# An mLSTM with an MLP behind it: Softplus and Erf on ScalarE, gate exponents read back from DRAM, a 512-token up projection, and a list schedule

## The chip, the cores and the metric

The kernel runs on one core of a Trainium2 chip. The metric is the device time of one execution in microseconds (us), less being better. The kernel before was run three times: 509.87, 509.98 and 510.92 us, median 509.98.

## What is computed

An mLSTM layer (batch 4, 8 heads, 768 tokens, head size 40) is followed by a two-layer MLP on all 3072 tokens. In short form (all data are float32; the weights reach the chip as float64 words):

```python
def _attn_ref(q, k, v, i_gate, f_gate, o_gate):
    ...
    for t in range(S):
        m_new = np.maximum(f_gate[:, :, t] + m, i_gate[:, :, t])
        f_stab = np.exp(f_gate[:, :, t] + m - m_new)
        i_stab = np.exp(i_gate[:, :, t] - m_new)
        C = f_stab[..] * C + i_stab[..] * np.einsum('bhd,bhe->bhde', vt, kt)
        n = f_stab[..] * n + i_stab[..] * kt
        denom = np.maximum(np.abs(nq), 1.0)          # nq = n . q
        o = 1.0 / (1.0 + np.exp(-o_gate[:, :, t]))
        y[:, :, t] = o * (C q) / denom

def _moe_ref(x, w_in, w_out):                        # x 3072 x 320
    h = x @ w_in                                     # 320 x 2048
    sp = np.maximum(h, 0.0) + np.log1p(np.exp(-np.abs(h)))   # softplus
    return (h * erf(sp)) @ w_out                     # 2048 x 320
```

## The kernel before

**Attention.** The 768 tokens are worked off in 6 chunks of `L` = 128. A step `s` is one chunk `c` of one batch `b`, so there are 24 steps. For a chunk, `gate_chunk` runs the scans of the gates on VectorE and leaves rows `x0`: a decayed input exponent, a decay exponent, and its exponential. To spread these rows over 128 partitions, each row is split into three bf16 parts and multiplied by rows of ones: L503 (and L505 in chunk 0) adds the two exponents in PSUM with 512 columns for half of the heads, ScalarE takes `Exp` into `dm` (L510), and GpSimd masks it. L548 does the same for the factor on `q` and on the state. The scores are L536 (32 small matmuls), the product with the mask is L526, the output `ph` is L564 and L568, and the state's increment `pk` is L579 from `vg`. `den` is the denominator, `y` is the gated output in `kvo`, written by L608 and L615. Three transposes (L624) turn `y` into columns; ScalarE copies the rounded part `xh` (L633), VectorE subtracts the remainder `xl` (L637). A pair of batches fills 256 tokens.

**MLP.** A group `g` is 1024 elements a partition: 4 column blocks `j` of `w_in` by 256 tokens; 48 groups do all. An operand is held as a rounded float32 part and a remainder, so an up block is eight matmuls of 256 columns for each `j` (L769). ScalarE copies `h` out of PSUM to `hb` (L779) and evaluates erf(softplus(h)) by an approximation of four `Tanh` passes and a `Square` (L785, L789, L793, L798, L810) with two passes on VectorE between them (L802, L806). VectorE multiplies by `h` (L814), rounds to `gh` (L819) and subtracts to `gl` (L824). The down block is three matmuls of 320 columns for each `j` and batch (L838, L839, L841) into the banks `po0` and `po1`; after the fourth group ScalarE scales them out (L847).

**Weights.** Each weight tile comes as pairs of 32-bit words; ScalarE and VectorE make float32 of them (L654, L659, L660, L662), ScalarE rounds (L667), and the remainder is taken by VectorE (L680) or, for `w_out`, by two matmuls with the identity (L674, L675) and a copy (L682). Raw words lie in MLP tiles that are not yet in use (`raw_tile`) or in tiles named `raw`.

**Order.** Every piece of work is put into a list with a time from tables of numbers (`ATT`, `MLP`, `LOAD`, `DECODE`, `GROUP_AT` and others), the list is sorted by that time, and this is the order of each engine's instructions. Each engine takes its instructions in this order and waits for what each one needs. SyncE (SP) issues all DMAs. PSUM has four banks for attention (`pa`), two for `h`, and one each for `po0` and `po1`.

```python
        def put(fn):
            plan.append((start + parts[part], len(plan), fn))
...
    with tc.manual_schedule():
        for _, _, fn in sorted(plan, key=lambda x: x[:2]):
            fn()
```

## Time and profile before

| what | value |
|---|---|
| time, median of 3 runs | 509.98 us (509.87 to 510.92) |
| span of the profiled execution | 508.03 us, 15222 instructions |
| that execution's own time | not listed apart from the three runs |
| ScalarE table loads | 1 |
| DMA | 39.48 MB, mean 78 GB/s |

The span is what the hardware profiler saw from the first to the last instruction; the time of a run is a little longer. PE is TensorE's matmuls and PEld its weight loads, DVE is VectorE, ACT is ScalarE, POOL is GpSimd. A page of the profile divides the span into 40 slices and gives each engine's busy share there; views of the trace give windows, groups of like instructions, and single rows. A row of the timeline is the start in us, the duration, the engine, the line, the operation with its output and inputs, and shapes. A group has the count behind an x, then its busy sum, the mean of one in ns, and the idle time before it.

### The profile page before, as it was taken

Reading aid. Unit: us, or ns where it says so; the run is one execution under the profiler, and the core shown is the slowest. Engines: PE = TensorE matmul, PEld = TensorE weight load, DVE = VectorE, ACT = ScalarE, POOL = GpSimd, SP = SyncE. Lnnn points to the kernel's source line nnn. Section 1 sums busy time; section 2 is a strip of 40 time slices with the busy share of each in tenths; the row PEclk is TensorE's granted clock in tenths of the full one; section 3 lists DMA queues with packets and bytes.
Section 4 is the critical chain, followed back from the end, with each engine's and each line's share of the span. In section 5 each row is a group of like instructions: output and inputs, shape, how many; then the busy total and the mean of one; then the engine's idle time right before and its main releaser. Section 6 shows DMA issues by size and latency. Waiting matters only on the chain.

```text
span 508.0 us, 15222 instructions
## 1 busy us (share of the span) xinstructions
PE 471.2 (93%) x6552; PEld 440.5 (87%) x6552; DVE 444.7 (88%) x695; ACT 382.5 (75%) x616; POOL 88.6 (17%) x112
## 2 busy tenths in 40 slices
PE   3647889998999999999999999999999999999996
PEld 2435689897998999999999999999999999999995
DVE  5879999999997989988989989989989878787873
ACT  6556889877778868868768878768769679678980
POOL 3212002113222113113013113013113013010000
PEclk9865899999999999999999999999999999999999
DMA  7949713303205012212113114104015004000000
GB/s 249 259 166 229 230 56 111 89 3 108 78 5 160 15 46 72 69 38 96 46 46 93 47 39 126 49 3 131 10 39 158 16 3 139 1 15 15 0 28 26
DMA packets 16811, 39.48 MB, mean 78 GB/s; under 512 B 2728, under 2 KB 7336, under 8 KB 16744
## 3 DMA queue, kind: packets, MB, share of 16 engines
q1 hardware_dynamic: 16744, 38.51, 26.2%
q8 instruction: 51, 0.84, 0.7%
q14 instruction: 16, 0.13, 0.1%
HBM read 33.40 MB, written 3.93 MB: 73 GB/s over the span
## 4 chain that ended last, share of the span: by engine, by line
PE 55%; DVE 23%; ACT 8%; DMA 7%; issue 4%; SPq 2%; DVEq 0%; ACTq 0%
PE h L769 22%; PE po L838 8%; PE po L841 7%; PE po L839 7%; PE pa L536 4%; DVE gl L824 3%; DVE n L802 3%; DVE hb L814 3%; DVE n L806 3%; DMA qk<-in_qk_dram 3%; PE pa L564 2%; PE pa L568 2%; DMA hb<-in_w_in_dram 2%; DVE gh L819 2%; ACT n L810 2%
## 5 line engine op out<-in xcount | busy, mean ns | idle before, releaser
L769 PE MATMUL h<-xh,wh 128*128 128x256 f32 x576 | 161.7, 286 | 1.2 <-ACT n L785 1.2
L769 PE MATMUL h<-xl,wh 128*128 128x256 f32 x576 | 160.2, 283 | 1.7 <-DVE xl L637 1.7
L838 PE MATMUL po<-woh,gh 128*128 128x320 f32 x384 | 123.5, 331 | 2.7 <-DVE gh L819 1.5
L839 PE MATMUL po<-wol,gh 128*128 128x320 f32 x384 | 114.6, 308 | 0.0
L769 PEld LDWEIGHTS h<-xh,wh 128*128 128x128 f32 x576 | 109.9, 191 | 2.3 <-ACT n L785 1.4
L769 PEld LDWEIGHTS h<-xl,wh 128*128 128x128 f32 x576 | 109.8, 191 | 2.3 <-DVE xl L637 2.2
L769 PE MATMUL h<-xh,wl 128*128 128x256 f32 x384 | 108.5, 283 | 0.0
L841 PE MATMUL po<-woh,gl 128*128 128x320 f32 x384 | 82.4, 315 | 0.8 <-DVE gl L824 0.8
L838 PEld LDWEIGHTS po<-woh,gh 128*128 128x128 f32 x384 | 72.4, 189 | 6.1 <-DVE gh L819 2.1
L839 PEld LDWEIGHTS po<-wol,gh 128*128 128x128 f32 x384 | 72.3, 188 | 1.2 <-issue 0.6
L769 PEld LDWEIGHTS h<-xh,wl 128*128 128x128 f32 x384 | 73.3, 191 | 0.0
L785 ACT ACTIVATE n<-h 128x512 f32<-128x512 f32 x96 | 57.8, 606 | 19.5 <-PE h L769 17.8
L618 POOL COPY kvo<-kvo 128x64 f32<-128x64 f32 x24 | 22.8, 950 | 258.5 <-DVE kvo L615 101.5
L814 DVE SCALAR_TENSOR_TENSOR hb<-n,hb 128x1024 f32<-128x1024 f32 x48 | 59.5, 1239 | 7.2 <-ACT n L810 6.9
L824 DVE TENSOR_TENSOR gl<-hb,gh 128x1024 fp32r<-128x1024 f32 x48 | 60.7, 1265 | 4.5 <-DVE gh L819 0.5
L841 PEld LDWEIGHTS po<-woh,gl 128*128 128x128 f32 x384 | 59.6, 188 | 1.6 <-DVE gl L824 1.2
L806 DVE SCALAR_TENSOR_TENSOR n<-n,n 128x1024 f32<-128x1024 f32 x48 | 58.9, 1228 | 2.3
L802 DVE SCALAR_TENSOR_TENSOR n<-n,hb 128x1024 f32<-128x1024 f32 x48 | 58.4, 1217 | 2.9 <-ACT n L793 2.9
L779 ACT ACTIVATE hb<-h 128x512 f32<-128x512 f32 x96 | 53.0, 604 | 10.1 <-DVE gl L824 10.1
L810 ACT ACTIVATE n<-n 128x1024 f32<-128x1024 f32 x48 | 50.8, 1058 | 10.5 <-DVE n L806 10.2
L514 POOL TENSOR_SCALAR_AFFINE_SELECT dm<-dm 128x512 f32<-128x512 f32 x48 | 44.9, 944 | 54.2 <-ACT dm L510 54.2
L793 ACT ACTIVATE n<-n 128x1024 f32<-128x1024 f32 x48 | 50.9, 1061 | 1.3
(92 smaller groups left out, 730.8 us busy)
## 6 DMA issues: line engine op xcount, KB each, us to landing
kvo<-in_kvo_dram SPq DMA_DIRECT2D x24, 484.0 KB
...
```

What stands on the lines that cost most here:

```text
L769: nc.tensor.matmul(v.h[n // 2][:, n % 2 * T:(n % 2 + 1) * T], w, m, start=(q == 0), stop=(q == len(ops) - 1))
L779: nc.scalar.activation(v.hb[:, hs], v.h[i], AF.Copy)
L785: nc.scalar.activation(v.a[:, hs], v.h[i], AF.Tanh, scale=PARAMS[0], bias=PARAMS[1])
L793: nc.scalar.activation(v.a, v.a, AF.Square, scale=PARAMS[6], bias=PARAMS[7])
L802: nc.vector.scalar_tensor_tensor(out=v.a, in0=v.a, scalar=PARAMS[8], in1=v.hb, op0=ALU.add, op1=ALU.mult)
L806: nc.vector.scalar_tensor_tensor(out=v.a, in0=v.a, scalar=PARAMS[9], in1=v.b, op0=ALU.mult, op1=ALU.add)
L810: nc.scalar.activation(v.a, v.a, AF.Tanh, scale=PARAMS[10], bias=PARAMS[11])
L814: nc.vector.scalar_tensor_tensor(out=v.hb, in0=v.a, scalar=1.0, in1=v.hb, op0=ALU.add, op1=ALU.mult)
L824: nc.vector.tensor_tensor(v.gl, v.hb, v.gh.bitcast(F32), op=ALU.subtract)
L838: nc.tensor.matmul(po[k, b], v.gh[:, ts], woh[:, w], start=(j == 0), stop=False)
L839: nc.tensor.matmul(po[k, b], v.gh[:, ts], wol[:, w], start=False, stop=False)
L841: nc.tensor.matmul(po[k, b], v.gl[:, ts], woh[:, w], start=False, stop=(j == NFF - 1))
```

## The change

Four parts are exchanged. The line numbers in this section are those of the changed kernel, where the piece is new.

**Gate exponents.** No bf16 split and no replication matmul is left. In a step of chunk 0 the rows are spread by 16 float32 matmuls with a column of the identity broadcast (L403, L404). From chunk 1 on, GpSimd and TensorE have no part in it: the decay rows and their exponentials are written to DRAM (`gd`) and read back replicated over the partitions, as `dm` and `eT`; the input exponent comes from one transpose of the rows (L354, `aT`) and is added by VectorE (L427) ahead of `Exp` (L431). VectorE multiplies `q` (L469) and the state (L503) by `eT`.

**Steps.** The denominator is four short VectorE passes; `y` is turned by two transposes and, for the last 64 columns, two float32 matmuls on halves of the array (L542, L544).

**MLP.** In chunk 0 a group is as before, 4 `j` by 256 tokens. From chunk 1 on it is 2 `j` by 512 tokens, all four batches at once (L691), with a PSUM bank `po` for each batch. ScalarE evaluates `Softplus` (L703) and `Erf` (L708); VectorE multiplies (L713), rounds (L717), subtracts (L721). `Exp`, `Softplus` and `Erf` lie in three table sets of ScalarE (X, S, G), and each change of the set is an instruction of its own, `ACT_TABLE_LOAD`, on ScalarE (L769): 59 in the program. Groups go in pairs: two groups' `Softplus`, a change of the set, their two `Erf`.

**Weights and order.** Raw words have three tiles of their own (`raw`) and are decoded in place; `w_in` and `w_out` come by quarters of the 2048 columns, and every second `w_out` block leaves its remainder to TensorE and ScalarE, the other to VectorE. The tables are gone: `Plan` gives each piece an engine, an estimated cost, and due times that follow backwards from a nominal time of each group, and simulates the engines to choose, at each moment, the piece with the earliest due time whose inputs and tiles are there.

```diff
-GROUP_EVERY = 14.1101
...
+class Plan:
...
+    LAT = {'PE': 0.15, 'ACT': 0.2, 'DVE': 0.15, 'POOL': 0.2, 'SP': 0.0}
+    SWITCH = 1.5
+    RATE = 240e3
...
+    def dues(self):
...
+        for _ in range(3):
+            for o in reversed(self.ops):
+                for s in o.succ:
...
+                    if phase < len(todo) and loaded != phase:
+                        k = self.kinds[phase]
+                        if loaded is None or self.kinds[loaded] != k:
+                            order.append((now, lambda k=k: switch(k)))
+                            free[e] = now + self.SWITCH
...
+                    if o.phase is not None and o.phase != phase or o.sets and self.kinds[loaded] not in o.sets:
+                        continue
...
+                    due = o.due - (1.0 if e == 'PE' and o.kind == mode else 0.0)
+                    if best is None or due < best[0]:
+                        best = (due, o)
...
+KIND = {'X': 'exp_and_others', 'S': 'softplus', 'G': 'sigmoid_and_others'}
+BATCHES = [[2, 2, 2, 2]] * 6
+SLOTS = dict(gt=1, m=2, x=2, aT=2, qk=2, kvo=2, dm=2, eT=1, vg=1, den=2, xh=2, xl=2, o=2,
+             raw=3, hb=4, n0=4, gh=2, gl=2, pa=2, h=2, gd=2, **{f'po{b}': 1 for b in range(B)})
+START = 30.0
...
+SLOW = 9.0
...
+def nominal(g):
+    return START + (SLOW * g if g < 8 else SLOW * 8 + EVERY * (g - 8))
+EVERY = 8.6
...
+    for c in range(NC):
+        g = 8 * c
+        for i, n in enumerate(BATCHES[c]):
+            if c + 1 < NC and i in XAT[c > 0]:
+                exps[c + 1][XAT[c > 0].index(i)] = plan.phase('X')
+            s = plan.phase('S')
+            e = plan.phase('G')
+            for j in range(n):
+                soft[g + j], erfs[g + j] = s, e
...
+            nc.tensor.transpose(p[:, 0:128], t['x', c][:, 0], ident)
...
+        @op('ACT', 0.22, r=[(('x', c), 0)], w=[(('x', c), 2)], phase=exps[c - 1][1])
+        def _():
+            nc.scalar.activation(t['x', c][:, 2], t['x', c][:, 1], AF.Exp)
...
+                    t['gd', c] = tc.dram_tile([2, B, H, L], F32, name=f"gd{c}")
+                nc.sync.dma_start(t['gd', c][:, b].rearrange("i h t -> h i t"), t['x', c][32 * b:32 * b + H, 1:3])
...
+                        k = 32 * b + 4 * i + h
+                        one = ident[:, k:k + 1].to_broadcast([128, 128])
+                        nc.tensor.matmul(p[:, h], one, t['x', c][:, 1], start=True, stop=False)
+                        nc.tensor.matmul(p[:, h], t['x', c][:, 0], one, start=False, stop=True)
...
+                    nc.scalar.activation(A('dm')[:, 4 * i:4 * i + 4], A(f'pb{i}').rearrange("p (h t) -> p h t", t=L), AF.Exp)
...
+            @dma(512, r=[(('gd', c), b)], w=[K('dm', 'e0'), K('dm', 'e1')], tile_=('dm', ('dm', s)))
+            def _():
+                nc.sync.dma_start(new('dm', [128, H, L], ('dm', s)).rearrange("p h t -> p (h t)"),
+                                  t['gd', c][0, b].rearrange("h t -> (h t)").partition_broadcast(128))
...
+                nc.sync.dma_start(e[0:64], src[0].partition_broadcast(64))
+                nc.sync.dma_start(e[64:QR], src[1].partition_broadcast(D))
...
+            @op('DVE', 1.18, r=[(('aT', c), 0)], w=[K('dm', 'e0'), K('dm', 'e1')])
+            def _():
+                nc.vector.tensor_tensor(A('dm'), A('dm'), bias().to_broadcast([128, H, L]), op=ALU.add)
...
+            @op('ACT', 0.95, w=[K('dm', 'e0'), K('dm', 'e1'), K('dm', 0), K('dm', 1)], phase=ph)
+            def _():
+                nc.scalar.activation(A('dm'), A('dm'), AF.Exp)
...
-                for p in range(NPR):
-                    nc.tensor.matmul(pq[:, p], selP[:, 2 * p:2 * p + 2].rearrange("p a b -> p (a b)"),
-                                     splB[b][:, 1, :], start=True, stop=True)
...
+            @op('DVE', 0.6, r=[K('eT')], w=[K('qk', 'q')])
+            def _():
+                q = A('qk')[0:QR, 0]
+                nc.vector.tensor_tensor(q, q, A('eT')[0:QR], op=ALU.mult)
...
+            nc.vector.tensor_copy(den, pv()[:, :, D])
+            nc.vector.scalar_tensor_tensor(out=den, in0=den, scalar=-1.0, in1=den, op0=ALU.mult, op1=ALU.max)
+            nc.vector.tensor_scalar(out=den, in0=den, scalar1=1.0, scalar2=2.0, op0=ALU.max, op1=ALU.mult)
+            nc.vector.reciprocal(den, den)
...
+            for i in range(2):
+                nc.tensor.transpose(p[:, i * L:(i + 1) * L], y[:, i * 128:(i + 1) * 128], ident)
+            for i in range(2):
+                nc.tensor.matmul(p[64 * i:64 * i + 64, 2 * L:3 * L], y[:, 256:320], ident, start=True, stop=True)
...
+        @op('DVE', n / 960 + 0.1, r=r, w=[(R, 1)])
+        def _():
+            nc.vector.tensor_scalar(out=raw()[:, :, 0], in0=raw()[:, :, 0], scalar1=29, scalar2=None,
+                                    op0=ALU.logical_shift_right)
...
+            lo_, hi_ = raw()[:, :, 0], raw()[:, :, 1]
+            nc.vector.scalar_tensor_tensor(out=lo_, in0=hi_, scalar=3, in1=lo_,
...
+            nc.vector.scalar_tensor_tensor(out=lo_, in0=hi_, scalar=-0x80000000, in1=lo_,
                                            op0=ALU.bitwise_and, op1=ALU.bitwise_or)
...
+        if by_dve:
+            @op('DVE', n / 960 + 0.1, r=[(R, 1), whi], w=[wlo])
...
+                nc.vector.tensor_tensor(lo(), word(0), hi().bitcast(F32), op=ALU.subtract)
+        else:
...
+            @op('PE', 0.85 * n / 320, r=[(R, 1), whi, ('ident', 0), ('nident', 0)], w=[(z, 0)], tile_=('pa', z), kind='a')
...
+            @op('ACT', n / 1200 + 0.06, r=[(z, 0)], w=[wlo])
...
+            raw_of[R] = raw(R, 2 * DM)
+            nc.sync.dma_start(raw_of[R], w_out.bitcast(I32)[j * 128:(j + 1) * 128])
...
+               ('woh', j), ('wol', j), j % 2 == 0)
...
+        js, bs = (range(4 * (q // 2), 4 * (q // 2) + 4), range(2 * (q % 2), 2 * (q % 2) + 2)) if c == 0 else \
+            (range(2 * q, 2 * q + 2), range(B))
...
+        per = 512 // N
...
+                    for k, (w, m) in enumerate(ops):
+                        nc.tensor.matmul(h[:, n * N:(n + 1) * N], w, m, start=(k == 0), stop=(k == len(ops) - 1))
...
+        @op('ACT', 0.95, r=[(('hb', g), 0), (('hb', g), 1)], w=[(('n0', g), 0)], tile_=('n0', ('n0', g)), phase=soft[g])
+        def _():
+            nc.scalar.activation(new('n0', [128, 1024], ('n0', g)), G('hb'), AF.Softplus)
...
+        @op('ACT', 0.95, w=[(('n0', g), 0)], phase=erfs[g])
...
+            nc.scalar.activation(n0, n0, AF.Erf)
...
+            nc.vector.tensor_tensor(n0, n0, G('hb'), op=ALU.mult)
...
+        for b in bs:
...
+                        if lo:
+                            nc.tensor.matmul(po, a[:, ts], woh[:, j], start=False, stop=(j == NFF - 1))
+                        else:
+                            nc.tensor.matmul(po, a[:, ts], woh[:, j], start=(j == 0), stop=False)
+                            nc.tensor.matmul(po, a[:, ts], wol[:, j], start=False, stop=False)
...
+    order = plan.run(nc.scalar.preload_act_table_set and (lambda k: nc.scalar.preload_act_table_set(KIND[k])))
...
     with tc.manual_schedule():
-        for _, _, fn in sorted(plan, key=lambda x: x[:2]):
+        for fn in order:
             fn()
```

On TensorE, late in the program, before: the last `L548` matmuls of a step, down blocks of two groups, and the next step's replication (`selP` and `splB` hold the selecting rows and the split exponents).

```order
L548 LDWEIGHTS selP
L548 MATMUL pa<-splB_81,selP 128x128
L841 MATMUL po_5787<-woh,gl 128x320 x2
L838 MATMUL po_5814<-woh,gh 128x320
L839 MATMUL po_5814<-wol,gh 128x320
L838 MATMUL po_5814<-woh,gh 128x320
L839 MATMUL po_5814<-wol,gh 128x320
L503 LDWEIGHTS splB_82
L503 MATMUL pa<-rhsE_79,splB_82 128x512
```

And at a like place after, between the state's increment and the next up block of 512 columns:

```order
L738 MATMUL po_3129<-woh,gl 128x320 x2
L740 MATMUL po_3226<-woh,gh 128x320
L741 MATMUL po_3226<-wol,gh 128x320
L740 MATMUL po_3226<-woh,gh 128x320
L741 MATMUL po_3226<-wol,gh 128x320
L738 MATMUL po_3137<-woh,gl 128x320 x2
L738 MATMUL po_3226<-woh,gl 128x320 x2
L542 MATMUL pa<-ident,kvo 128x128 x2
L544 MATMUL pa<-ident,kvo 64x128 x2
L691 MATMUL h<-xh,wh 128x512
```

The replication matmuls are gone from the row, the down blocks of two batches stand together, the transposes are two and two, and an up matmul has 512 columns.

On ScalarE, in the last third of the program, before: passes of several groups and of attention stand mixed.

```order
L798 ACTIVATE n1_3859<-hb_3790 128x1024
L785 ACTIVATE n0_3867<-h_3797 128x512
L510 ACTIVATE dm_3920<-pa_3833 128x512
L633 ACTIVATE xh_3940<-pa_3845 128x3x128
L779 ACTIVATE hb_3962<-h_3797 128x512
L779 ACTIVATE hb_3962<-h_3778 128x512
L429 ACTIVATE x0_3704<-x0_3704 128x128
L785 ACTIVATE n0_3867<-h_3778 128x512
L510 ACTIVATE dm_3984<-pa_3943 128x512
L603 ACTIVATE den_3986<-pa_3871 128x8
L810 ACTIVATE n0_3682<-n0_3682 128x1024
```

After, in the last third too: a pair of groups with its two changes of the table set (`n0` holds the function's value, `hb` the copy of `h`).

```order
L551 ACTIVATE xh_3913<-pa_4471 128x3x128
L699 ACTIVATE hb_4517<-h_4499 128x512
L699 ACTIVATE hb_4517<-h_4564 128x512
L703 ACTIVATE n0_4623<-hb_4517 128x1024
L699 ACTIVATE hb_4673<-h_4649 128x512
L551 ACTIVATE xh_3913<-pa_4668 128x3x128
L699 ACTIVATE hb_4673<-h_4675 128x512
L703 ACTIVATE n0_4697<-hb_4673 128x1024
L769 ACT_TABLE_LOAD
L708 ACTIVATE n0_4623<-n0_4623 128x1024
L708 ACTIVATE n0_4697<-n0_4697 128x1024
L769 ACT_TABLE_LOAD
```

The passes `L785`, `L789`, `L793`, `L798` and `L810` are gone; the two `Erf` of a pair stand together behind its two `Softplus`, with a table load ahead of each kind.

On VectorE, up to the remainder `xl` of the last step of chunk 1 (the eighth such row of the program), before:

```order
L806 SCALAR_TENSOR_TENSOR n_1923<-n_1923,n_2110 128x1024
L608 SCALAR_TENSOR_TENSOR kvo<-kvo,pa 128x320
L598 TENSOR_TENSOR state_87<-state_87,pa 40x4x41
L612 TENSOR_SCALAR den<-den 128x8
L613 RECIPROCAL den<-den 128x8
L615 TENSOR_TENSOR kvo<-kvo,den 128x320
L814 SCALAR_TENSOR_TENSOR hb<-n_1923,hb 128x1024
L598 TENSOR_TENSOR state_87<-state_87,pa 40x4x41
L819 CAST gh<-hb 128x1024
L824 TENSOR_TENSOR gl<-hb,gh 128x1024
L802 SCALAR_TENSOR_TENSOR n_2112<-n_2112,hb 128x1024
L637 TENSOR_TENSOR xl<-pa,xh 128x3x128
```

After, the rows up to the same piece:

```order
L522 COPY den<-pa 128x8
L523 SCALAR_TENSOR_TENSOR den<-den 128x8
L524 TENSOR_SCALAR den<-den 128x8
L525 RECIPROCAL den<-den 128x8
L530 SCALAR_TENSOR_TENSOR kvo<-kvo,pa 128x320
L535 TENSOR_TENSOR kvo<-kvo,den 128x320
L503 TENSOR_TENSOR state_72<-state_72,eT 104x328
L564 TENSOR_SCALAR raw<-raw 128x320
L515 TENSOR_TENSOR state_72<-state_72,pa 40x4x41 x2
L574 SCALAR_TENSOR_TENSOR raw<-raw 128x320
L576 SCALAR_TENSOR_TENSOR raw<-raw 128x320
L555 TENSOR_TENSOR xl<-pa,xh 128x3x128
```

Before, whole groups of the MLP (`L814`, `L819`, `L824`) stand ahead of that row, and the decoding is behind VectorE; now the decoding of `w_out` (`raw`, `wol`) is still going on between the passes of the step. The row now has number 237 of VectorE's program, before 252.

More of the change, by code (lines that the diff above doesn't have):

```diff
@@ L25 @@
 V1 = D + 1
[L27 to L29 removed]
+T = B * L
 KV = DM + H * V1
@@ L375, in setup @@
-    def setup():
+    state = [cp.tile([128, NPR, 2 * V1], F32, name=f"state{b}") for b in range(B)]
+    wh = cp.tile([128, 3, DFF], F32R, name="wh")
+    wl = cp.tile([128, 2, DFF], F32R, name="wl")
+    woh = cp.tile([128, NFF, DM], F32R, name="woh")
+    wol = cp.tile([128, NFF, DM], F32R, name="wol")
+    @dma(6, w=[('cst', 0)], due=-100.0)
+    def _():
         nc.sync.dma_start(cst, consts)
+    @op('POOL', 2.0, w=[('ident', 0)])
+    def _():
         make_identity(nc, ident)
+    @op('ACT', 0.2, r=[('ident', 0)], w=[('nident', 0)])
@@ L390, in tile_mlstm_moe, with _ @@
-    spls = {}
+    for b in range(B):
+        @op('POOL', 0.5, w=[('st', b)])
+        def _(b=b):
+            nc.gpsimd.memset(state[b], 0.0)
+    exps = [[None, None] for _ in range(NC)]
+    soft, erfs = {}, {}
+    exps[0] = [plan.phase('X')] * 2
+    for c in range(NC):
[7 more added lines that the diff above has]
+                soft[g + j], erfs[g + j] = s, e
+            g += n
@@ new lines, in attention, with _ @@
+        for j in range(2):
+            @op('POOL', 0.95, w=[K('dm', j)])
+            def _(j=j):
+                nc.gpsimd.affine_select(out=dm()[:, j], in_=dm()[:, j], pattern=[[0, NPR], [1, L]],
+                                        compare_op=ALU.is_ge, fill=0.0, base=0, channel_multiplier=-1)
+        if not last:
+            @op('DVE', 0.42, r=[K('dm', 0), K('dm', 1), K('kvo', 'v')], w=[K('vg')], tile_=('vg', ('vg', s)))
+            def _():
+                vg = new('vg', [128, H, V1], ('vg', s))
+                nc.vector.tensor_tensor(vg, v1(), A('dm')[:, :, L - 1:L].to_broadcast([128, H, V1]), op=ALU.mult)
@@ L532, in _ @@
+        @op('PE', 1.05, r=[K('qk', 'q'), K('qk', 'k')], w=[K('S0'), K('S1')], tile_=[('pa', ('S0', s)), ('pa', ('S1', s))], kind='a', due=due,
+            after=[K('dm', 0), K('dm', 1)] + ([] if last else [K('vg')]))
+        def _():
+            x = [new('pa', [128, 512], (f'S{j}', s)).rearrange("p (n t) -> p n t", t=L) for j in range(2)]
+            q, k = A('qk')[:, 0], A('qk')[:, 1]
             for p in range(NPR):
@@ L605, in _ @@
-        @at('yg')
+            @op('DVE' if c else 'ACT', 0.5, r=[K('pk')], w=[('st', b)])
+            def _():
+                for j in range(2):
+                    js = slice(64 * j, 64 * j + D)
+                    so = st[js, :, j * V1:(j + 1) * V1]
+                    pk = A('pk')[:, 0:NPR * V1].rearrange("p (n d) -> p n d", d=V1)[js]
+                    if c == 0:
+                        nc.scalar.activation(so, pk, AF.Copy)
+                    else:
+                        nc.vector.tensor_tensor(so, so, pk, op=ALU.add)
@@ new lines, in tile_mlstm_moe, with raw, weights_in @@
+    pair = lambda raw: raw.rearrange("p (n w) -> p n w", w=2)
+    homes = ['raw']
+    def raw(key, n):
+        tag = homes[raws.setdefault(key, len(raws)) % len(homes)]
+        shape = [128, 1024] if tag == 'raw' else [128, 3, T]
+        x = new(tag, shape, key, F32R).bitcast(I32)
+        return (x if tag == 'raw' else x.rearrange("p a b -> p (a b)"))[:, 0:n]
+    raws, raw_of = {}, {}
+    home = lambda key: (homes[raws.setdefault(key, len(raws)) % len(homes)], key)
+    def weights_in(part, k):
+        R = ('raw', part, k)
+        @dma(512, w=[(R, 0)], tile_=home(R))
+        def _():
+            raw_of[R] = raw(R, 1024)
+            nc.sync.dma_start(raw_of[R],
+                              w_in.bitcast(I32)[k * 128:(k + 1) * 128, part * 1024:(part + 1) * 1024])
+        cs = slice(part * 512, (part + 1) * 512)
+        decode(R, lambda: pair(raw_of[R]), 512, lambda: wh[:, k, cs], lambda: wl[:, k, cs], [(R, 0)],
+               ('wh', k, part), ('wl', k, part), True)
```

998 lines of the change are left out of this document (379 added, 619 removed).

## The prediction

> **What bounds the kernel now.** I read the busy line of the page first, then the stages by window, then single rows of TensorE's timeline for its pace, then the groups for the prices of VectorE and ScalarE.
>
> ```profile
> PE 471.2 (93%) x6552; PEld 440.5 (87%) x6552; DVE 444.7 (88%) x695; ACT 382.5 (75%) x616; POOL 88.6 (17%) x112
> 0.00:8.00 8.00, 0.00 (x0) 0.00 (x0) 3.54 (x11) 3.37 (x6) 3.01 (x16) 1.00 0.68 230
> 8.00:35.00 27.00, 16.97 (x297) 11.33 (x297) 21.32 (x45) 16.30 (x38) 5.22 (x8) 0.83 0.84 233
> 35.00:110.00 75.00, 65.42 (x816) 58.00 (x817) 72.80 (x132) 60.21 (x115) 9.90 (x14) 0.88 0.45 127
> 160.00:320.00 160.00, 158.16 (x2318) 150.70 (x2317) 148.19 (x233) 125.96 (x193) 34.11 (x36) 1.00 0.24 70
> 320.00:480.00 160.00, 159.84 (x2218) 153.69 (x2218) 137.51 (x192) 125.32 (x191) 23.43 (x25) 1.00 0.15 43
> ```
>
> The columns of a window are its length, then PE, PEld, DVE, ACT and POOL busy, TensorE's clock, DMA share and GB/s. There are two regimes. From 35 to 110 us VectorE is busy 72.80 of 75 (97%): the start-up, with the decoding of the weights, is VectorE's. From 160 to 480 us TensorE is busy 318.0 of 320: there the kernel is as long as TensorE's work. VectorE at 89% and ScalarE at 79% follow. So a pass that leaves VectorE or ScalarE pays only in the first 110 to 150 us; later only TensorE's work and its waits count.
>
> TensorE's busy time overstates a matmul, since the ends overlap. Its pace is the distance from start to start:
>
> ```profile
> 309.13 0.28 PE L769 MATMUL h<-xh,wh 128*128 128x256 f32 x1
> ...
> 311.01 0.39 PE L503 MATMUL pa<-rhsE,splB 128*128 128x512 bf16 x1
> 291.12 0.31 PE L838 MATMUL po<-woh,gh 128*128 128x320 f32 x1
> ...
> 292.88 0.31 PE L838 MATMUL po<-woh,gh 128*128 128x320 f32 x1
> 293.56 1.10 PE L536 MATMUL pa<-qk 40*64 40x128 f32 x32
> 294.59 0.35 PE L564 MATMUL pa<-state,qk 104*32 104x82 f32 x8
> ...
> 295.80 0.48 PE L579 MATMUL pa<-vg,kvo 128*32 128x41 f32 x32
> 296.21 0.41 PE L838 MATMUL po<-woh,gh 128*128 128x320 f32 x1
> 301.24 0.39 PE L503 MATMUL pa<-rhsE,splB 128*128 128x512 bf16 x1
> 301.28 0.50 PE L838 MATMUL po<-woh,gh 128*128 128x320 f32 x1
> 301.62 0.31 PE L839 MATMUL po<-wol,gh 128*128 128x320 f32 x1
> 302.06 0.49 PE L624 MATMUL pa<-ident,kvo 128*128 128x128 f32 x3
> 302.30 0.39 PE L838 MATMUL po<-woh,gh 128*128 128x320 f32 x1
> 302.53 0.31 PE L839 MATMUL po<-wol,gh 128*128 128x320 f32 x1
> ```
>
> Sixteen up matmuls of 256 columns fill 309.13 to 311.01: 0.1175 us each, 0.459 ns a column. Twelve down matmuls of 320 fill 291.12 to 292.88: 0.147 each, 0.458 ns a column. An attention step needs 1.03 (scores, L536), 1.21 (L564 and L568), 0.41 (L579) and 0.33 (the three transposes: 0.47 from 302.06 to 302.53, less one down matmul). One replication matmul L503 costs 0.23 (0.38 from 301.24 to 301.62, less 0.147); there are two in a step.
>
> How far is reality from such sums? One period of eight MLP groups and four steps:
>
> ```profile
> 233.21 0.44 ACT L847 ACTIVATE o_sb<-po 128x320 f32<-128x320 f32 x1
> 307.78 0.44 ACT L847 ACTIVATE o_sb<-po 128x320 f32<-128x320 f32 x1
> 382.35 0.44 ACT L847 ACTIVATE o_sb<-po 128x320 f32<-128x320 f32 x1
> ```
>
> It takes 74.57 us, twice. The sum is 8 x (32 x 0.1175 + 24 x 0.147) = 58.3, plus 4 x 2.98 = 11.9, plus the exponents' matmuls, 4 x 0.46 for L503 and some 0.9 for the small L548: 72.9. So 2.3% is lost in a period where TensorE never starves. I carry that 2.3% over.
>
> **The change, part by part.** *TensorE after the start-up.* From the first 512-token matmul of chunk 1 on, the new order holds 640 up matmuls of 512 columns, 1008 down matmuls (two groups of chunk 0 are still open) and 16 attention steps. At 0.459 ns a column the up part is 640 x 0.235 = 150.4, exactly what 1280 of 256 cost: wider tiles alone win nothing. The rows allow 0.1169 to 0.1181 and 0.1458 to 0.1475 for the two widths, so 0.228 to 0.240 for 512, 4 us either way; L503's 512 columns took 0.23. I take 0.235. The Trainium skill, "TensorE: Matmul & The Clock Gate", section "Back-to-back issue gap", gives N/2.4 + 2.5 ns, which is 216 ns for 512; by it the sum would be 12 us shorter. The trace disagrees where it can be tested: by that rule 256 columns take 109 ns, measured 117.5. Downs: 1008 x 0.147 = 148.2. Attention: L503 and L548 go; one transpose becomes two f32 matmuls on halves of the array, so I take 0.44 for 0.33: 16 x (1.03 + 1.21 + 0.44) + 12 x 0.41 (the last chunk stores no state) = 47.8. Together 346.4, with 2.3% on it **354.4 us**.
>
> *When that begins.* These matmuls take all four batches at once, so they wait for the eighth L555 (`xl` of chunk 1's last step). VectorE's order has that row far behind, and VectorE is the start-up's engine, so I add up all that stands ahead of it there:
>
> ```profile
> L814 DVE SCALAR_TENSOR_TENSOR hb<-n,hb 128x1024 f32<-128x1024 f32 x48 | 59.5, 1239 | 7.2 <-ACT n L810 6.9
> L824 DVE TENSOR_TENSOR gl<-hb,gh 128x1024 fp32r<-128x1024 f32 x48 | 60.7, 1265 | 4.5 <-DVE gh L819 0.5
> L819 DVE CAST gh<-hb 128x1024 fp32r<-128x1024 f32 x48 | 35.5, 739 | 3.4 <-DVE hb L814 0.9
> L526 DVE TENSOR_TENSOR dm<-pa,dm 128x512 f32<-128x512 f32 x48 | 31.8, 684 | 2.8 <-PE pa L536 2.4
> L637 DVE TENSOR_TENSOR xl<-pa,xh 128x384 fp32r<-128x384 f32 x24 | 13.1, 547 | 1.4 <-ACT xh L633 1.4
> L615 DVE TENSOR_TENSOR kvo<-kvo,den 128x320 f32<-128x320 f32 x24 | 11.8, 492 | 0.8
> L659 DVE TENSOR_SCALAR bits<-bits 128x320 int32<-128x320 int32 (+1 forms) x26 | 10.3, 394 | 0.9 <-ACT bits L654 0.9
> L662 DVE SCALAR_TENSOR_TENSOR bits<-raw,bits 128x320 int32<-128x320 int32 x16 | 8.9, 555 | 0.5
> L680 DVE TENSOR_TENSOR wl<-bits,wh 128x512 fp32r<-128x512 f32 x8 | 5.2, 682 | 0.0
> ```
>
> Decoding: 26 shifts x 0.39, 32 combining passes of 320 at 0.53 (L662 and, a little less, its neighbour), 20 of 512 at 0.69, 10 subtractions at 0.68 and 7 at 0.43 (by columns): 50.7. Seven MLP groups, of which each has now one product, one cast and one subtraction: 7 x 1.24 + 7 x 0.74 + 6 x 1.27 = 21.5. Eight steps: 2 x 0.68 + 0.49 + 0.49 + 0.55 = 2.89 each, 23.1. New: five bias additions over 1024 columns at 1.27 (nearest row L824), and four q products at 0.68: 9.1. Some 88 short passes (denominators, `vg`, state, gates), none over L615's 0.49, estimated at 0.28: 25. Sum **129 us**. Two passes a group (L802, L806) are gone from here, but the four batches wait for two steps more than a pair did.
>
> Its idle time comes on top. By the first windows VectorE stood idle 10.1 of the first 35 us, and 2.2 of the next 75. With that the row comes at 129 + 10 + 3 = 142. Three things add to it in the new order. The first scores stand behind 32 f32 matmuls (L403, L404) where one bf16 L503 and four L505 did per half; I estimate 3. Raw weights have three homes, where they had whole MLP tiles besides, so a load starts when the tile three before it is decoded: 3. And the first product waits behind a pair of groups, a table load and Erf: 2. I take **150 us**; ends 140 (no added idle, short passes at 0.26) and 163.
>
> *ScalarE.* Six passes a group become four (two copies, Softplus, Erf): L785 and two 1024-wide passes go. But the functions sit in three table sets, and the order holds 58 table loads after the first.
>
> ```profile
> 0.80 1.28 ACT L378 ACT_TABLE_LOAD   x1 [0.80 <-PEq L922]
> 2.10 0.31 ACT L378 ACTIVATE nident<-ident 128x128 fp32r<-128x128 f32 x1
> L779 ACT ACTIVATE hb<-h 128x512 f32<-128x512 f32 x96 | 53.0, 604 | 10.1 <-DVE gl L824 10.1
> L789 ACT ACTIVATE n<-n 128x1024 f32<-128x1024 f32 x48 | 50.4, 1051 | 0.1
> ```
>
> A load took 1.28 and the next pass began 0.02 later. So a pair of groups costs 4 x 0.60 + 4 x 1.05 + 2 x 1.28 = 9.2 of the 14.6 us that TensorE needs for it: ScalarE is no bound. Its latency is the question, since groups now go in pairs. From the second group's last up matmul to the first group's first down matmul: copy 0.60, Softplus 1.05, load 1.28, Erf 1.05, product 1.24, cast 0.74, and about 0.1 for each of three handovers: 6.3. TensorE's order leaves one down block (24 x 0.147) and one up block (16 x 0.235) between them: 7.3. It fits, with 1.0 to spare. Where attention passes of VectorE or a `th` of ScalarE stand in between, the spare is used up. I add 3 us for that (0 to 20).
>
> *The end.* The last pair has only one down block (3.5) for cover against 6.3: 2.8. After the last matmuls:
>
> ```profile
> 504.05 0.75 PE L841 MATMUL po<-woh,gl 128*128 128x320 f32 x4
> 504.88 0.44 ACT L847 ACTIVATE o_sb<-po 128x320 f32<-128x320 f32 x1 [3.13 <-PE po L841]
> ```
>
> Four of 0.147 end at 504.6, the span (508.03) 3.4 later; that stays.
>
> *Readback.* Per step 720 KB more are loaded (`dm` 512, `eT` 208): 1.6 MB every 18 us is 90 GB/s, against 230 moved in the first windows. I cost it at nothing; the cover is one half chunk, about 35 us.
>
> Sum: 150 + 354.4 + 3 + 2.8 + 3.4 = 513.6 of span. The profiled run's time lies 1.95 above its span (509.98, the median of the three, against 508.03): **515.5 us**, 1.1% slower.
>
> **The rivals.** *VectorE is freed early (faster).* If the list order leaves VectorE no idle time beyond that of before, the eighth L555 comes at 142, and the pair latency stays hidden: 515.5 - 8 - 3 = 504.5 us. It decides at the time of that one row: before 144.5 us, all else as summed, the kernel is faster. For it speaks that 2.4 us of passes a group are gone there; against it that the three-home weights and in-order waits on ScalarE are new. Chance 0.25.
>
> *A cost per matmul, not per column (faster, little).* Then 512 columns take 0.228 by the rows: 511 us; chance 0.05. Only the page's gap would make it 503.
>
> *Table loads drain the engine.* The one load of the trace stood at an idle engine. If a load must wait out the pass before it and the pass behind it starts late, a switch grows by up to two passes (2.1); at 1.7 the pair's latency is 8.0, 0.7 over its cover, for 24 pairs 17 us: 532. For it speaks that no row shows a switch between passes. Chance 0.11. The Trainium skill, "ScalarE: Activation LUTs", section "What ACT_TABLE_LOAD costs", has 1283 ns, as the row here, and 1380 ns of drain for each switch; by that the latency is 7.7 and the time about 525. No run here shows the drain yet.
>
> *The readback is late.* SP's queue is in order: four small writes wait for the gate's Exp, the `dm` and `eT` loads behind them for the writes, and `qk`, `kvo` and stores queue behind those. If that is exposed once a chunk, at 2.2 us for 512 KB at 233 GB/s, as much for the write and a wait in the Exp phase, some 5 us for five chunks: 540. For it: ScalarE's Exp phase holds Softplus back while it waits. Against: the cover of 35 us. Chance 0.07.
>
> **How the numbers follow.** Forecast 0.52 (509.5 to 524), the rivals 0.25, 0.05, 0.11 and 0.07. From no added idle and the lower matmul price (499.5) to the drain's case (533) lies 0.8 of it. Within 0.2%, which is about what a measurement of this kernel can tell from no change, lies the lower edge of the forecast and the upper of the first rival: 0.08. Faster 0.27, slower 0.65.
>
> **What would show it.** The eighth L555 at 150, and VectorE over 80% busy up to it; 512-column starts 0.235 apart; TensorE over 95% busy from 160 on; 58 loads of 1.28 with the next pass 0.02 to 0.1 behind; the last up block about 13 us before the end of TensorE. I am wrong if TensorE has gaps of several us in each chunk (drain or readback), or if the 512-wide matmuls begin well before 142.

## The result, and the profile after

The changed kernel takes 534.03 us (median of 4 runs, 533.4 to 534.07), the kernel before 509.93 in the same runs: a ratio of 1.048, 95% interval 1.045 to 1.051. It is slower, as forecast, but by 24 us and not by 5.5; the range ended at 533.0.

The page's busy line of the changed kernel, and the windows of the prediction once more (length, then PE, PEld, DVE, ACT, POOL busy, TensorE's clock, DMA share, GB/s):

```profile
PE 483.9 (91%) x5933; PEld 418.4 (79%) x5933; DVE 354.6 (67%) x607; ACT 318.1 (60%) x430; POOL 51.8 (10%) x60
8.00:35.00 27.00, 22.58 (x395) 20.67 (x394) 18.59 (x43) 12.44 (x26) 5.14 (x8) 0.92 0.74 206
35.00:110.00 75.00, 60.81 (x731) 54.37 (x734) 59.47 (x120) 47.13 (x73) 4.04 (x4) 0.80 0.50 148
110.00:160.00 50.00, 38.00 (x636) 30.69 (x633) 44.37 (x89) 28.93 (x47) 4.37 (x6) 0.90 0.53 158
0.00:155.00 155.00, 120.15 (x1755) 105.47 (x1755) 119.67 (x252) 89.56 (x146) 14.59 (x29) 0.87 0.54 161
160.00:320.00 160.00, 157.75 (x2017) 134.78 (x2016) 110.21 (x176) 100.30 (x126) 21.16 (x18) 1.00 0.33 94
320.00:480.00 160.00, 158.01 (x1904) 135.35 (x1903) 99.88 (x155) 101.78 (x127) 15.12 (x13) 1.00 0.26 77
```

VectorE and ScalarE have 90 and 64 us less to do than before, TensorE 13 more, and from 160 us on TensorE is busy 315.8 of 320 again. The difference lies ahead: from 35 to 110 us VectorE is busy 59.5 of 75, where it was 72.8, and TensorE 60.8 for 65.4, at a clock of 0.80 for 0.88. In the start-up no engine is full.

TensorE's rows where the 512-column work begins, and in its steady pace; the bracket is idle time before the row and what ended it:

```profile
155.21 0.50 PE L691 MATMUL h<-xh,wh 128*128 128x512 f32 x1 [0.59 <-ACT xh L551]
156.95 0.65 PE L691 MATMUL h<-xl,wh 128*128 128x512 f32 x1 [1.25 <-DVE xl L555]
157.40 0.63 PE L691 MATMUL h<-xh,wl 128*128 128x512 f32 x1
157.82 0.63 PE L691 MATMUL h<-xh,wh 128*128 128x512 f32 x1
...
271.95 0.40 PE L691 MATMUL h<-xh,wh 128*128 128x512 f32 x1
...
275.70 0.31 PE L740 MATMUL po<-woh,gh 128*128 128x320 f32 x1
```

The second row waits for the eighth `xl`. Sixteen matmuls of 512 columns fill 271.95 to 275.70: 0.234 each, the summed 0.235. By the formula in the Trainium skill, "TensorE: Matmul & The Clock Gate", section "Back-to-back issue gap", it would be 0.216. The section gives this formula for a single matmul, and about 131 ns at 512 columns for a stream of them; the trace agrees with neither, and decides.

### The profile page after: what moved, and what is told of

It reads as the page before. It is cut to its first block, busy times and chain, and to the rows that moved or that the text cites. A ratio compares the mean times of both kernels' runs of the same rounds, so it can differ in the third digit from the quotient of the medians.

```text
span 531.7 us, 13705 instructions
## 1 busy us (share of the span) xinstructions
PE 483.9 (91%) x5933; PEld 418.4 (79%) x5933; DVE 354.6 (67%) x607; ACT 318.1 (60%) x430; POOL 51.8 (10%) x60
## 4 chain that ended last, share of the span: by engine, by line
PE 62%; DVE 23%; ACT 9%; issue 4%; DMA 2%; SPq 0%; DVEq 0%; ACTq 0%
PE h L691 30%; PE po L740 7%; PE po L738 7%; PE po L741 7%; DVE n L713 4%; PE pa L454 3%; DVE gl L721 3%; ACT L769 2%; PE pa L482 2%; DVE gh L717 2%; DVE raw L576 2%; PE pa L486 2%; DVE raw L574 2%; ACT n L703 2%; ACT n L708 2%
## 5 line engine op out<-in xcount | busy, mean ns | idle before, releaser
L691 PE MATMUL h<-xh,wh 128*128 128x512 f32 (+1 forms) x336 | 128.0, 383 | 2.2 <-ACT xh L551 1.2
L691 PE MATMUL h<-xl,wh 128*128 128x512 f32 (+1 forms) x336 | 125.3, 376 | 1.3 <-DVE xl L555 1.2
L713 DVE TENSOR_TENSOR n<-n,hb 128x1024 f32<-128x1024 f32 x48 | 58.6, 1220 | 82.5 <-ACT n L708 82.5
L691 PE MATMUL h<-xh,wl 128*128 128x512 f32 (+1 forms) x224 | 84.1, 375 | 0.4 <-DVE wl L586 0.4
L691 PEld LDWEIGHTS h<-xh,wh 128*128 128x128 f32 x336 | 66.9, 199 | 15.6 <-issue 2.9
L691 PEld LDWEIGHTS h<-xl,wh 128*128 128x128 f32 x336 | 66.9, 199 | 10.5 <-DVE xl L555 1.9
L721 DVE TENSOR_TENSOR gl<-n,gh 128x1024 fp32r<-128x1024 f32 x48 | 60.8, 1267 | 3.1
L703 ACT ACTIVATE n<-hb 128x1024 f32<-128x1024 f32 x48 | 50.9, 1059 | 1.5
L691 PEld LDWEIGHTS h<-xh,wl 128*128 128x128 f32 x224 | 44.8, 200 | 8.0 <-DVE wl L586 0.7
L708 ACT ACTIVATE n<-n 128x1024 f32<-128x1024 f32 x48 | 49.1, 1053 | 0.2
L717 DVE CAST gh<-n 128x1024 fp32r<-128x1024 f32 x48 | 35.8, 746 | 2.7
```

The lines of the kernel that those rows point to most:

```text
L691: nc.tensor.matmul(h[:, n * N:(n + 1) * N], w, m, start=(k == 0), stop=(k == len(ops) - 1))
L703: nc.scalar.activation(new('n0', [128, 1024], ('n0', g)), G('hb'), AF.Softplus)
L708: nc.scalar.activation(n0, n0, AF.Erf)
L713: nc.vector.tensor_tensor(n0, n0, G('hb'), op=ALU.mult)
L717: nc.vector.tensor_copy(new('gh', [128, 1024], ('gh', g), F32R), G('n0'))
L721: nc.vector.tensor_tensor(new('gl', [128, 1024], ('gl', g), F32R), G('n0'), G('gh').bitcast(F32), op=ALU.subtract)
```

## The experiments

All times are medians; the kernel before took 509.5 to 510.8 us beside them. The runs of one variant lie 1 to 6 us apart, so a difference of 2 or 3 us between two variants is not clear of the noise. "Same order" means that every engine's instructions stand as in the changed kernel; where it isn't said, the planner made a new order. Times of single rows, such as the eighth `xl`, are from one profiled run each. "..." in an edit stands for lines that are not shown.

**Table loads** (58 `ACT_TABLE_LOAD` left out)

```diff
-            nc.scalar.activation(new('n0', [128, 1024], ('n0', g)), G('hb'), AF.Softplus)
+            nc.scalar.activation(new('n0', [128, 1024], ('n0', g)), G('hb'), AF.Tanh)
...
-            nc.scalar.activation(n0, n0, AF.Erf)
+            nc.scalar.activation(n0, n0, AF.Tanh)
...
+        if not loaded:
+            loaded.append(nc.scalar.preload_act_table_set(KIND['X']))
...
+    order = plan.run(switch)
```

> The order of every engine is that of the changed kernel; its 58 table loads after the first are left out, and Softplus and Erf are both replaced by Tanh, which the first table set holds (so the MLP's function is another). Theory 'loads hidden': the pair's latency stays under TensorE's cover after the start-up, so only the last pair (one load, 1.3 us) and a part of the five loads that stand on the start-up's chain (6.4 us) come back: 526 to 532 us. Rival 'loads on the path' (each switch of a pair delays TensorE): 24 pairs behind the start-up give back 12 us or more: under 520 us. Rival 'no load on any path': 532.5 to 534 us.

Measured 527.41 us. The eighth `xl` comes 3.6 us earlier, the wait ahead of the last group falls from 2.7 to 1.3, and the rest of TensorE's stage wins 1 us. After the start-up the loads are hidden, as the forecast had it; all 58 together cost 6.6 us (the four runs without them took 525.4 to 530.1).

**A pass of the decoding** (`L576` left out)

```diff
-            nc.vector.scalar_tensor_tensor(out=lo_, in0=hi_, scalar=-0x80000000, in1=lo_,
-                                           op0=ALU.bitwise_and, op1=ALU.bitwise_or)
```

> Same order; the last of the two combining passes of the decoding (26 passes, 15.5 us of VectorE before 156 us) is left out, so the weights lose their signs. Theory 'VectorE's ledger' (the prediction's): the eighth xl comes earlier by nearly all of the passes that stand ahead of it, 12 to 15 us, and the time is 519 to 522 us. Rival 'hand to hand' (VectorE and TensorE wait for each other in turn, and neither is the bound): only the passes on the chain count, at most 9 us, and PE's part of the chain stays: 526 to 532 us.

Measured 526.55 us: 15.5 us of VectorE gave 7.5. The eighth `xl` comes at 146.8; up to it VectorE is busy 105.6 us, where it was 120.9, and idle 41.2, where it was 35.4. So a third of what was taken off came back as idle time, and VectorE alone is not the start-up's bound. That the rest stood on a chain that changes engines fits, but this run does not show the chain.

**Pairs of batches in chunk 1**

```diff
-            (range(2 * q, 2 * q + 2), range(B))
+            (range(4 * (q % 4), 4 * (q % 4) + 4), range(2 * (q // 4), 2 * (q // 4) + 2)) if c == 1 else \
+            (range(2 * q, 2 * q + 2), range(B))
```

> Chunk 1's MLP in groups of 4 column blocks by 256 tokens, first two batches first, as the kernel before had it; chunks 2 to 5 on 512 tokens. Theory 'four-batch barrier': TensorE, which stood idle 11 us between 110 and 156 us, takes the first pair's groups from the sixth xl on (119.9 us in the changed kernel), and the time falls by 8 to 12 us: 522 to 526 us. Rival 'VectorE's ledger': the passes of those groups go ahead of the steps of the second pair on VectorE and only change places with them: 531 to 535 us.

Measured 526.05 us. The wait for all four batches at the start of chunk 1 costs 8 us: the eighth `xl` comes only 1.8 us earlier (154.5), but 68 up matmuls of the chunk's first pair now stand ahead of it. In the kernel before it came later still, and did not hold TensorE up, which was busy 48.2 of 50 us from 110 to 160: there, too, the first pair went ahead. This row before, then in the changed kernel:

```profile
164.60 0.55 DVE L637 TENSOR_TENSOR xl<-pa,xh 128x384 fp32r<-128x384 f32 x1
```
```profile
156.34 0.56 DVE L555 TENSOR_TENSOR xl<-pa,xh 128x384 fp32r<-128x384 f32 x1
```

**Turning y as before**

```diff
+            nc.gpsimd.tensor_copy(p[:, 320:384], p[:, 256:320])
...
-            for i in range(2):
+            for i in range(3):
                 nc.tensor.transpose(p[:, i * L:(i + 1) * L], y[:, i * 128:(i + 1) * 128], ident)
-            for i in range(2):
-                nc.tensor.matmul(p[64 * i:64 * i + 64, 2 * L:3 * L], y[:, 256:320], ident, start=True, stop=True)
```

> Same order; the two transposes and two half-array matmuls of a step are replaced by three transposes from a padded tile, as before, with a GpSimd copy of 64 columns. Theory 'dearer turning': 0.70 us of TensorE a step against 0.24 is 0.46 for each of the 16 steps behind the start-up, 7.4 us, and up to 2 us more in the start-up: 524.5 to 527 us. Rival 'the copy's hop counts as much': GpSimd's copy stands between VectorE's product and the transposes and delays them by as much as they win: 532 to 536 us.

Measured 531.76 us, 2.3 less: between the two, and with runs from 530.8 to 534.7 not clear of the changed kernel's 533.4 to 534.1. In the profiled run TensorE's attention rows behind the start-up fall from 54.0 to 50.9 us, but its waits and small losses grow from 19.2 to 22.0, so that stage wins nothing (371.3 for 371.6 us); the eighth `xl` comes 2.3 us earlier.

**Half of chunk 0's replication** (`L404` left out)

```diff
-                        nc.tensor.matmul(p[:, h], t['x', c][:, 0], one, start=False, stop=True)
```

> Same order; of the 64 float32 replication matmuls of chunk 0 the 32 that add the input exponent (L404) are left out, so chunk 0's exponents lack it. Theory 'replication on the chain': 64 of them take 17.5 us of TensorE ahead of 31 us, and the first scores stand behind 32 of them; half of them gone brings the steps of chunk 0, and with them the eighth xl, 4 to 8 us earlier: 526 to 530 us. Rival 'weights set the start' (the first up matmuls wait for VectorE's decoding and the DMAs whatever TensorE does): 532 to 535 us.

Measured 534.22 us: nothing. The first 512-column matmul starts 1.2 us earlier, and the end is where it was; the 32 matmuls that went are not on the path that matters.

**The planner's costs from the profile**

```diff
-    SWITCH = 1.5
+    SWITCH = 1.3
...
-            @op('ACT', 0.49, r=[((f'h{i}', g), 0)], ...
+            @op('ACT', 0.6, r=[((f'h{i}', g), 0)], ...
```

> The planner is given the durations that the profile of the changed kernel has (copies 0.60 for 0.49, Softplus, Erf and Exp 1.06 for 0.95, 1024-wide VectorE passes 1.25 for 1.18, casts 0.75 for 0.66, the mask 1.07 for 0.95, products 0.68 for 0.62, combining passes longer, a table load 1.3 for 1.5); nothing else changes, the order follows. Theory 'order on too cheap costs': each engine's order fits the chip better, the hand-to-hand waits of the start-up shrink, and the time falls by 4 to 10 us: 524 to 530 us. Rival 'order not the cause': 531 to 538 us.

Measured 536.46 us. Truer costs alone don't help: in the new order the first 512-column matmul starts 11 us later, at 166.2, and what follows it is 8 us shorter.

**256 tokens in all chunks**

```diff
-            (range(2 * q, 2 * q + 2), range(B))
+            (range(4 * (q % 4), 4 * (q % 4) + 4), range(2 * (q // 4), 2 * (q // 4) + 2))
```

> All chunks behind the first in groups of 4 column blocks by 256 tokens, pairs of batches as before: the 512-token part undone, all else kept. Theory 'columns count, not matmuls': behind the start-up 256-column matmuls at 0.1175 us cost what 512-column ones at 0.235 cost, and the barrier of four batches is gone as in the run with pairs in chunk 1 alone (526.05 us): 523 to 529 us. Rival 'wide tiles win behind the start-up': 4 us or more above that run, 530 us or more.

Measured 528.67 us: with the 512-token part undone 5.4 us faster than the change, and 2.6 slower than pairs in chunk 1 alone, which is within the noise. Wide tiles win nothing that shows: columns count, not matmuls, as the paces of 0.1175 and 0.234 us say too.

**Pairs, turning and a shorter last batch together** (the edits for pairs and for turning, and this one)

```diff
-BATCHES = [[2, 2, 2, 2]] * 6
+BATCHES = [[2, 2, 2, 2]] * 5 + [[2, 2, 2, 1, 1]]
```

> Pairs in chunk 1, three transposes, and the last two groups each as a pair's half (batches 2, 2, 2, 1, 1), so that the last group's latency has no second Erf ahead of it. If the gains add up: 534.0 less 8.0, less 2.3, less 1 to 2 us: 521.5 to 523 us. If the transposes' gain is eaten where VectorE is late: 524 to 527 us.

Measured 520.87 us. They add up, within the spread of the runs (517.7 to 523.8).

**Homes for raw weights**

```diff
-    homes = ['raw']
+    homes = ['raw', 'raw', 'raw', 'n0', 'hb']
...
```

> The changed kernel with raw weights in five homes instead of three: every fourth raw tile takes an n0 tile and every fifth an hb tile, as the kernel before put raw words into idle MLP tiles; the planner orders anew. Theory 'weights late' (in the changed kernel the last quarter of w_in is rounded at 131.5 us, before it was at 65.8, and TensorE's last two groups of chunk 0 begin at 134.6, right behind): the quarters come earlier and the time falls by 6 to 11 us: 523 to 528 us. Rival 'homes do not count' (VectorE has no time for an earlier decoding): 531 to 535 us.

Measured 522.24 us: 11.8 us, the largest single part. A home is a tile that raw words are loaded into. SyncE's waits up to 155 us in the changed kernel, and with five homes (line of the DMA, what freed it, us in total, times, longest; L659 and L657 are the same load of `w_out`):

```profile
SPq L659 <- PE pa L593: 23.3, 3, 9.2
...
SPq L659 <- DVE hb L586: 7.7, 1, 7.7
SPq L659 <- DVE wl L586: 5.5, 5, 2.5
```
```profile
SPq L657 <- PE pa L593: 4.4, 1, 4.4
```

SyncE stood 23.3 us until TensorE's remainder matmul (`L593`), the last reader of every second `w_out` tile, had read a raw tile. That matmul stands in TensorE's order behind other work, and every later load in SyncE's queue stands behind the load that waits.

**No wait for later quarters**

```diff
                 for n, j in enumerate(mine):
+                    j = j % 4 if c == 0 else j
...
```

> Same order; chunk 0's MLP multiplies all four quarters by the first quarter's weights (so chunk 0's output is another), all decoding stays: TensorE waits for no later quarter. Theory 'weights late': the groups that began at 97.8 and 134.6 us begin earlier, and a part of TensorE's idle time before 155 us goes: 522 to 528 us. Rival 'VectorE and order': the decoding stands in VectorE's order ahead of the eighth xl as before, and TensorE's rows stand behind the steps': the first 512-column matmul comes no earlier, 531 to 535 us.

Measured 537.30 us. TensorE's own wait for the weights is not the point; the first 512-column matmul comes only 1.7 us earlier, at 153.5. What is left is the other way, by VectorE's order, where the decoding of late words stands ahead of the attention passes; this run does not show it, the next two bear on it. Behind the start, TensorE's attention rows take 57.1 us for 54.0, and the run is 3 us longer than the changed kernel; the reason is open.

**Fewer and more homes**

```diff
-             raw=3, ...
+             raw=2, ...
```

> The changed kernel with two raw tiles instead of three. Theory 'homes': SyncE's queue stood 36 us before 156 us in the changed kernel for a raw tile to come free (behind it wait all other loads); with one home less that grows, and the time rises by 10 to 16 us: 544 to 550 us. Rival 'the five-homes run won by another order only': within 4 us of the changed kernel, 530 to 538 us.

```diff
-    homes = ['raw']
+    homes = ['raw', 'raw', 'raw', 'n0']
...
```

> The changed kernel with a fourth home (every fourth raw tile in an n0 tile). Theory 'homes': most of the gain of five homes (11.8 us) is there with the first one: 523 to 527 us. Rival: 530 to 538 us.

Measured 559.42 us with two, 25 more and not 10 to 16, and 522.99 with four. The rounding of `w_in` by ScalarE (durations, then first and last start) in the kernel before, with two, three and four homes (of the four, one tile of `wh` comes from `n0` and has a row of its own):

```profile
L667 ACT ACTIVATE wh<-bits x8: 631/633/644, 14.2 to 65.8; 128x512 fp32r<-128x512 f32 x8
```
```profile
L581 ACT ACTIVATE wh<-raw x8: 662/688/711, 24.2 to 153.9; 128x512 fp32r<-128x512 f32 x8
```
```profile
L581 ACT ACTIVATE wh<-raw x8: 658/664/688, 24.8 to 131.5; 128x512 fp32r<-128x512 f32 x8
```
```profile
L581 ACT ACTIVATE wh<-raw x7: 652/667/689, 24.4 to 118.6; 128x512 fp32r<-128x512 f32 x7
```

And VectorE (the third busy time) from 35 to 110 us with two and with four homes:

```profile
35.00:110.00 75.00, 54.27 (x670) 47.77 (x671) 51.23 (x103) 38.79 (x61) 3.93 (x4) 0.79 0.39 120
```
```profile
35.00:110.00 75.00, 61.35 (x839) 54.66 (x841) 64.80 (x125) 53.72 (x85) 5.81 (x6) 0.87 0.58 166
```

Two, three, four, five homes: 559.4, 534.0, 523.0, 522.2 us, with VectorE busy 51.2, 59.5, 64.8, 64.9 (five) of 75. The four traces agree on where the time goes. Up to the eighth `xl` VectorE is busy alike in all (119.5, 120.9, 120.9 and 119.0 us), but idle 57.8, 35.4, 26.8 and 26.5, and that row comes at 177.3, 156.3, 147.6 and 145.5 us. Only a part of this idle time is a wait for raw words themselves: up to 156 us 11.0, 4.4, 0.9 and 1.5; most of the rest stands behind other engines. Each number of homes has an order of its own, so no single step leaves the order out; but three steps go one way. It is the number of homes; from four on something else binds. Which reader holds the home is not shown: SyncE waited for `L593` 23.9, 23.3, 15.8 and 4.4 us, which does not follow the times.

**Due times, and all parts together.** The first variant's due times (EVERY and SWITCH too, as its expectation says):

```diff
-START = 30.0
-LAG = 22.0
-XAT = ((2, 3), (0, 2))
-STEP = ((4.5, 5.5, 6.5, 7.5), (1.0, 2.0, 5.0, 6.0))
-SLOW = 9.0
+START = 47.6
+LAG = 21.5
+XAT = ((2, 3), (1, 2))
+STEP = ((5.81, 5.72, 7.21, 10.0), (0.96, 2.48, 5.03, 5.29))
+SLOW = 9.85
```

> Pairs in chunk 1, three transposes, every fourth raw tile in a gl tile, last batches 1, 2, 2, 2, 1, and other nominal times for the planner (START 47.6, LAG 21.5, SLOW 9.85, EVERY 8.16, other STEP, SWITCH 1.8). If the start-up's order is what costs the changed kernel its time, this comes well under the run with the first three alone (520.87 us): 495 to 510 us, below the kernel before. If TensorE's work behind the start-up is the bound (372 us from 155 us on): 515 us or more.

The second variant, by another set of due times:

> As the run before it, with raw tiles in five homes, batches of 3, 3, 2 groups in chunk 0, smaller batches at the ends of later chunks, START 89.6, LAG 22.6, SLOW 9.67, EVERY 6.72. Same theories: 495 to 510 us, or 515 us and more.

The first variant's due times alone:

> The changed kernel with the planner's nominal times of the fastest variant alone (START 47.6, LAG 21.5, SLOW 9.85, EVERY 8.16, its STEP, XAT and SWITCH); three homes, four-batch groups from chunk 1 on, its own transposes. Theory 'parts, not times': the later due times do not help while homes and the four-batch start bind: 528 to 536 us. Rival 'due times': 10 us or more come from them: 524 us or less.

All parts with the due times of the changed kernel:

> Pairs in chunk 1, three transposes, last batches 2, 2, 2, 1, 1, five homes, the planner's times as in the changed kernel. If the gains add: 520.9 less 11.8, 508 to 511 us, level with the kernel before; what the fastest variant (503.56) has below that is the due times'. If homes and pairs win the same microseconds (both fill TensorE's idle time ahead of the eighth xl): 514 to 518 us.

Measured: 503.56 us (ratio to before 0.988, 0.985 to 0.991), 510.12 (1.001, 0.999 to 1.004), 545.40 for the first one's times alone, 514.25 for all parts without them. Homes and pairs partly win the same microseconds (6.6 beyond the 520.87, not 11.8). The due times, a `gl` home in place of two others and another last batch bring 11 us together on top of the parts; no run has the due times alone there. Without the parts they cost 11, which neither theory foresaw. The eighth `xl` explains it (the times alone, then the fastest variant):

```profile
165.43 0.56 DVE L555 TENSOR_TENSOR xl<-pa,xh 128x384 fp32r<-128x384 f32 x1 [2.64 <-ACT xh L551]
```
```profile
164.66 0.56 DVE L555 TENSOR_TENSOR xl<-pa,xh 128x384 fp32r<-128x384 f32 x1
```

In both that row comes 8 to 9 us later than in the changed kernel. With the times alone the first 512-column matmuls wait for it and begin at 166.1, 11 us later. In the fastest variant 128 up matmuls of chunk 1's first pair stand ahead of it. In that variant:

```profile
35.00:110.00 75.00, 62.04 (x754) 55.79 (x753) 66.57 (x136) 55.98 (x90) 5.40 (x7) 0.90 0.55 165
110.00:160.00 50.00, 49.83 (x779) 47.04 (x781) 43.05 (x80) 29.68 (x43) 6.11 (x9) 0.93 0.40 120
```

From 110 us on TensorE is full, where the changed kernel had it busy 38.0 of these 50 us.

## Why the prediction was wrong

Span and time of the profiled run, 531.7 and 533.4 us, against the summed 513.6 and 515.5, term by term:

| term | forecast | measured |
|---|---|---|
| first 512-column matmul | 150 | 155.2 |
| up and down columns behind it | 150.4 + 148.2 | 150.4 + 148.2 (counts times pace) |
| attention rows | 47.8 | 54.0 |
| the 2.3% | 8.0 | 8.0 |
| waits over 0.15 us, the last pair's among them | 3 + 2.8 | 11.2 |
| after the last matmul | 3.4 | 4.7 |
| outside the span | 1.95 | 1.7 |

(Measured: the distance from start to start of each matmul from 155.21 to 526.81 us. For an up or down matmul the forecast pace of its kind is taken off, so these columns agree by their making; the pace itself is borne out by the 0.234 above. What is left over counts as a wait where it is over 0.15 us, else as small losses. What a row of attention takes counts as attention.) The 8.0 is luck: with the line drawn at 0.10 us it would be 3.2, and the waits 16.0. The two together are 19.2 us, where 13.8 were summed.

No rival came, and behind the start-up the mechanism was right: TensorE is full, its columns cost what was summed, and the loads, but for the last pair's, and the readback do not hold it up. Ahead of it the mechanism was wrong: VectorE was to be the bound, and it was not. The steps that failed are the idle time of VectorE ahead of the eighth `xl`, put at 21 us and measured 35, the 0.44 us for the turning matmuls, and the waits, 5.8 for 11.2. Each fell short on the same side, and the range took in no case where several do.

*The start.* The eighth `xl` at 156.3 lies inside the bounds, but two errors cancel in it. The ledger of VectorE's passes was right row by row: 254 rows up to there last 131.8 us in all, for 129, and the short ones 0.30 each, for 0.28. But one row often begins before the last one has ended, so they fill only 120.9 us of busy time; a sum of durations is too long by 10.9. And VectorE stood idle 35.4, not 21. The mis-sized term is **"raw weights have three homes ...: 3"**: a fourth home takes 8.6 us off VectorE's idle time, and 11 us off the whole. I read "a load starts when the tile three before it is decoded" as VectorE's delay, but for every second `w_out` block a tile is free only when TensorE, too, has read it, and SyncE's queue holds all other loads behind the one that waits. The 3 us for the float32 replication have no run behind them; half of it left out gave nothing. "VectorE is the start-up's engine" was true of the kernel before and not of this one. From 0 to 155 us TensorE's granted clock was 0.87, where it was 0.91 before; the prediction has no term for that, and no run here sets it apart.

*Attention.* The four turning matmuls were put at 0.44 us:

```profile
227.82 0.40 PE L691 MATMUL h<-xl,wh 128*128 128x512 f32 x1
228.06 0.38 PE L542 MATMUL pa<-ident,kvo 128*128 128x128 f32 x2
228.37 0.44 PE L544 MATMUL pa<-ident,kvo 128*64 128x128 f32 x4
228.74 0.50 PE L691 MATMUL h<-xh,wh 128*128 128x512 f32 x1
229.08 0.40 PE L691 MATMUL h<-xl,wh 128*128 128x512 f32 x1
```

From 228.06 (0.235 behind the first row) to 228.85 (0.235 ahead of the last) is 0.79 us. (Each half-array matmul is two records here.) As the table counts, from start to start, the turning takes 0.70 a step, 11.2 us in 16 steps where 7.0 were summed: 4.1 of the 6.2 us. Most of the rest is the scores, 18.0 us for 16.5. The 0.44, one transpose more than the three of before, had no row behind it.

*Waits.* TensorE's from 156 us on:

```profile
PE po L740 <- DVE gh L717: 2.7, 1, 2.7
PE pa L542 <- DVE kvo L535: 2.1, 6, 0.9
PE h L691 <- DVE xl L555: 1.2, 1, 1.2
PE h L691 <- ACT hb L699: 1.1, 1, 1.1
PE pa L482 <- DVE qk L469: 0.8, 1, 0.8
```

The first is the last pair's, forecast at 2.8. Behind the start-up no pair before it waits for its `gh`: the latency of 6.3 us is covered, as summed. The others are attention's hand-overs to VectorE, one late copy of `h` by ScalarE, and the start of the stage. There the granted clock was 0.52 from 157 to 160 us, and the first 512-column matmuls stand 0.42 us apart from 157.40 on; seven of them lose some 1.4 us in all.

*Tables.* The drain did not come:

```profile
285.62 1.06 ACT L703 ACTIVATE n<-hb 128x1024 f32<-128x1024 f32 x1
286.69 1.28 ACT L769 ACT_TABLE_LOAD   x1
287.99 1.06 ACT L708 ACTIVATE n<-n 128x1024 f32<-128x1024 f32 x1
```

The load starts 0.01 us behind the pass before it, and the next pass starts 0.02 us behind the load; the other 57 loads start as close behind a pass, and all but two are followed as closely. By the Trainium skill, "ScalarE: Activation LUTs", section "What ACT_TABLE_LOAD costs", 1380 ns of drain come on top; this trace shows none.

*The end.* The last copies wait for one of two `o` tiles, which a store holds:

```profile
526.37 0.75 PE L738 MATMUL po<-woh,gl 128*128 128x320 f32 x4
527.44 0.44 ACT L746 ACTIVATE o<-po 128x320 f32<-128x320 f32 x1 [1.02 <-DMA out_dram<-o]
528.33 0.44 ACT L746 ACTIVATE o<-po 128x320 f32<-128x320 f32 x1 [0.45 <-DMA out_dram<-o]
```

I took the old end over, where one batch came last; now two come within 1 us. *Readback* appears in no wait of TensorE, as forecast.

What stays open: how the waits of the start-up divide among the engines' orders, which reader of a home costs the most, what the lower clock there costs, and why the turning matmuls take twice the time of three transposes.
